# Dilated window attention beside a long convolution on one core: key offsets on partitions, v read back from DRAM at four shifts, sums by 32-column tiles, and spectra without a swapped copy

## The chip, the core and the metric

The kernel runs on one core of one Trainium2 chip. Time is device time in microseconds (us); each kernel was run several times, and the median stands with its range. The kernel before takes 244.41 us (three runs, 243.86 to 246.95). On the chips of the later runs its median lay between 244.3 and 247.2, so a kernel is compared with the runs of the kernel before on the same chip. A kernel that got a single look has one time, and its state (fast or slow) is unknown; it decides something only where the difference is far above the 1 to 2% by which runs scatter.

## The reference

Two independent parts share their length (S = 2048), their width (D = 576) and the output, where they stand side by side.

```python
# part A: 32 heads of 18, a causal window of 8 keys with step 2
qkv = x @ wqkv
idx = pos[:, None] - arange(8) * 2          # keys t, t-2, ..., t-14
logits = einsum(q, k[idx]) * 18 ** -0.5     # masked where idx < 0
o = einsum(softmax(logits), v[idx]);  a = o @ wo
# part B: a convolution of 4 taps, then one as long as the sequence, by FFT of length 4096
kv = (short convolution of k with shift_k) * v
y  = irfft(rfft(kv) * rfft(ssm_k))[:S] + kv * ssm_D;  b = q * y
out = concat(a, b)
```

## The kernel before

The engines each have a queue, and a written order (302 steps) says in which sequence the steps of A and B are issued. Three parts matter here.

**The weighted sum of v.** Times stand on the partitions (t = 16 a + b, with a on partitions). v is kept once in on-chip memory (`vX`), with a halo of 14 rows that is copied between partitions; the eight keys of a time are slots of the free axis. VectorE forms weight times v, and TensorE adds the eight products while it transposes them: each 128 x 128 block of products is loaded as weights and multiplied by the identity.

```python
def p_mul(tp, u):                                  # 16 of these
    vs = vX[:, t2:t2 + 15, :].rearrange(...)[:, 0:15:2]            # 8 keys, step 2
    nc.vector.tensor_tensor(P..., vs[:, :, 0:16], at.to_broadcast([128, W, 16, H]), ALU.mult)
    nc.vector.tensor_tensor(tails..., vs[:, :, 16:18], at.to_broadcast([128, W, 2, H]), ALU.mult)
def p_sum(tp, u):
    for ct in range(4):
        for wi in range(W):
            nc.tensor.matmul(oaccs[tp][:, u, ct, :], P[:, wi, 128 * ct:128 * ct + 128], ident[:], ...)
    # ... cut: the same for the tails
```

**The logit sum** multiplies products of q and shifted k by a 0/1 table on 32-column tiles of the array, four tiles at a time, reading its moving operand in runs of two elements (`prr[...][:, :, c, :, 2 * j:2 * j + 2]`).

**The spectra of B.** Transforms of the filter and of kv go out to DRAM (`Dk`, `Dx`) and come back with another axis on the partitions. A matmul makes 64 real and 64 imaginary rows at once. For the complex product, the filter's spectrum is also needed with its halves exchanged; two DMAs on GpSimd's queue make that copy.

```python
def by_rt(Dd, dh, g):
    return Dd[dh].rearrange("r (l h) d -> (r l) h d", h=32)[:, 8 * g:8 * g + 8, :]
def w_load(Dd, key, i):                            # 8 of Dk, 8 of Dx
    nc.sync.dma_start(Wr.get((key, i)), by_rt(Dd, i // 4, i % 4))
def k_spec(i):
    s2(Wr[("k", i)], i % 4, Kc[:, 0], 1.0 / 2048)
    nc.gpsimd.dma_start(Kc[0:64, 1], Kc[64:128, 0])
    nc.gpsimd.dma_start(Kc[64:128, 1], Kc[0:64, 0])
def g_prod(i, hv):
    nc.vector.tensor_tensor(Pp..., Kr[i][:, :, 4 * hv:4 * hv + 4, :], Xr[i]...to_broadcast([128, 2, 4, HD]), ALU.mult)
```

## Time and profile before

| | before |
|---|---|
| time, span of the profiled run | 244.41 us, 241.2 us |
| TensorE (PE) busy | 219.0 us, 91% of the span |
| VectorE (DVE) busy | 205.9 us, 85% |
| ScalarE (ACT) busy | 159.4 us, 66% |
| DMA | 55.24 MB, 229 GB/s over the span |

The prediction below shows the busy lines, stretches, groups and chain on which it was built. Two more views of the kernel before: the first is the busy time of the two halves (stretch, its length, then the busy time of each engine, the granted clock of TensorE as a share of full speed, the mean busy share of the 16 DMA engines, and GB/s). The second is the list of DMA issues, whose last column is the median time from issue to landing.

```profile
0.00:115.00 115.00, 104.73 (x807) 59.70 (x808) 102.40 (x125) 83.93 (x107) 11.04 (x38) 1.00 0.66 206
115.00:238.00 123.00, 114.32 (x1208) 88.96 (x1205) 103.47 (x108) 75.48 (x125) 14.52 (x24) 1.00 0.86 254
```

```profile
area<-Dk SPq DMA_DIRECT2D x8, 576.0 KB, 4.9
...
Dy<-area SPq DMA_DIRECT2D x8, 576.0 KB, 4.2
out_dram<-area SPq DMA_DIRECT2D x16, 288.0 KB, 4.4
```

In both halves TensorE is above 90%, and in the second the DMA engines are already busy 86% of the time.

### The profile page before, as it was taken

To read this page: it belongs to the slowest core of one execution; us is meant where nothing else is said; L and a number is where in the kernel's file an instruction comes from. 1 tells how busy PE (TensorE), PEld (TensorE's weight loads), DVE (VectorE), ACT (ScalarE), POOL (GpSimd) and SP (SyncE) were. 2 spreads that over 40 slices of the span, in tenths; PEclk is the share of its full clock that TensorE was granted. 3 is DMA by queue.
4 is the path that set the end of the run, shared out by engine and by line. 5 is a ranking of instruction groups with operands and counts; after the bars stand their busy time and mean duration, and the time that the engine had idled before them with its cause. 6 is when DMAs were issued, how large, how long until landed. Compare 5 with 4: busy or idle time off the path is not lost.

```text
span 241.2 us, 4997 instructions
## 1 busy us (share of the span) xinstructions
PE 219.0 (91%) x2013; PEld 148.7 (62%) x2013; DVE 205.9 (85%) x232; ACT 159.4 (66%) x231; POOL 25.6 (11%) x62
## 2 busy tenths in 40 slices
PE   1998999999996998999999779999899999999991
PEld 1444564446555544495684368768596779779770
DVE  1989999999988798998997999999999579974443
ACT  2777966779686777758837919858979682663030
POOL 8900000000000000000112010101120111111000
PEclk9999999999999999999999999999999999999998
DMA  6999994533435665557689887978879989879984
GB/s 206 323 339 388 362 288 146 157 101 99 134 91 169 196 195 148 169 141 281 192 226 283 273 237 257 269 246 272 181 258 284 280 237 281 273 227 283 282 241 147
DMA packets 44366, 55.24 MB, mean 229 GB/s; under 512 B 2316, under 2 KB 37468, under 8 KB 44344
## 3 DMA queue, kind: packets, MB, share of 16 engines
q1 hardware_dynamic: 42374, 47.71, 63.7%
q0 software_dynamic: 1968, 7.23, 11.2%
q8 instruction: 15, 0.25, 0.5%
q14 instruction: 7, 0.06, 0.1%
q10 hardware_dynamic: 2, 0.00, 0.0%
HBM read 29.27 MB, written 18.87 MB: 200 GB/s over the span
## 4 chain that ended last, share of the span: by engine, by line
PE 65%; DVE 12%; ACT 12%; DMA 6%; issue 4%; DVEq 0%; SPq 0%; ACTq 0%
PE psA L393 11%; ACT area L96 8%; PE psA L632 7%; PE psA L651 4%; PE psB L380 4%; DVE area L618 4%; PE psB L429 3%; PE psA L516 3%; PE psB L563 3%; PE psB L651 3%; PE psA L380 3%; PE psB L596 3%; PE psB L393 3%; ACT IAt L96 3%; DVE area L500 2%
## 5 line engine op out<-in xcount | busy, mean ns | idle before, releaser
L96 ACT ACTIVATE area<-psB 128x576 bf16<-128x576 f32 (+6 forms) x121 | 82.3, 714 | 33.6 <-PE psB L596 10.3
L96 ACT ACTIVATE area<-psA 128x576 bf16<-128x576 f32 (+7 forms) x94 | 66.9, 739 | 38.4 <-PE psA L651 11.6
L500 DVE TENSOR_TENSOR area<-area 128x2048 bf16<-128x2048 bf16 x32 | 38.0, 1224 | 2.9 <-PE psA L516 2.7
L618 DVE TENSOR_TENSOR area<-area,area 128x4096 bf16<-128x4096 bf16 x16 | 36.6, 2286 | 3.9 <-PE psA L632 3.3
L632 PE MATMUL psA<-ident,area 128*128 128x128 bf16 x512 | 34.0, 219 | 0.0
L632 PEld LDWEIGHTS <-area 128*128 128x128 bf16 x512 | 31.2, 98 | 1.8 <-DVE area L618 0.2
L393 PE MATMUL psA<-area,area 128*128 128x512 bf16 x120 | 31.3, 399 | 0.3 <-ACT area L96 0.3
L393 PEld LDWEIGHTS <-area 128*128 128x128 bf16 x160 | 15.5, 100 | 18.1 <-issue 1.9
L582 DVE TENSOR_TENSOR area<-area,area 128x2304 bf16<-128x2304 bf16 x16 | 21.5, 1355 | 2.6 <-DMA area<-area 1.1
L460 DVE TENSOR_TENSOR area<-area,area 128x2304 bf16<-128x2304 bf16 x16 | 21.3, 1353 | 0.6 <-DMA area<-in_B_k_dram 0.4
L574 POOL DMA_DIRECT2D area<-area x8 | 4.2, 527 | 159.0 <-DVE area L539 104.5
L380 PEld LDWEIGHTS <-area 128*128 128x128 bf16 x160 | 19.9, 144 | 1.2 <-issue 0.6
L563 PE MATMUL psB<-area,W 128*128 128x288 bf16 x96 | 18.0, 285 | 2.6 <-DVE area L98 1.6
L563 PEld LDWEIGHTS <-W 128*128 128x128 bf16 x128 | 11.9, 97 | 12.9 <-issue 10.0
L651 PEld LDWEIGHTS <-area 128*128 128x128 bf16 x160 | 15.5, 98 | 4.5 <-issue 0.6
L98 DVE CAST area<-psA 128x768 bf16<-128x768 f32 (+4 forms) x14 | 11.5, 834 | 6.3 <-PE psA L651 4.2
L429 PEld LDWEIGHTS <-T 128*128 128x128 bf16 x96 | 8.5, 98 | 12.9 <-issue 5.2
L465 DVE TENSOR_TENSOR area<-area 128x2304 bf16<-128x2304 bf16 x12 | 16.2, 1354 | 0.2
L596 PEld LDWEIGHTS <-IAt 128*128 128x128 bf16 x128 | 12.1, 97 | 6.6 <-issue 2.4
L429 PE MATMUL psB<-area,T 128*128 128x384 bf16 x60 | 14.0, 327 | 1.5 <-DVE area L290 1.2
L596 PE MATMUL psB<-area,IAt 128*128 128x288 bf16 x80 | 12.5, 285 | 1.0 <-DVE area L582 0.7
L651 PE MATMUL psA<-wv,area 128*128 128x288 bf16 x90 | 13.1, 286 | 0.0
(121 smaller groups left out, 287.3 us busy)
## 6 DMA issues: line engine op xcount, KB each, us to landing
Dx<-area SPq DMA_DIRECT2D x16, 288.0 KB, 3.0
Dk<-area SPq DMA_DIRECT2D x16, 288.0 KB, 3.1
area<-Dk SPq DMA_DIRECT2D x8, 576.0 KB, 4.9
area<-Dx SPq DMA_DIRECT2D x8, 576.0 KB, 4.6
area<-area POOLq DMA_DIRECT2D x16, 288.0 KB, 5.3
Dy<-area SPq DMA_DIRECT2D x8, 576.0 KB, 4.2
out_dram<-area SPq DMA_DIRECT2D x16, 288.0 KB, 4.4
area<-Dy SPq DMA_DIRECT2D x8, 576.0 KB, 6.3
```

Of the source, the lines that this page charges most:

```text
L96: nc.scalar.activation(dst, src, ACT.Copy, **({} if scale is None else {"scale": scale}))
L380: nc.tensor.matmul(ps[:, di, 0:288], xTt[:, kb, t2, :], wv[:, kb, d0:d1], start=(kb == 0), stop=(kb == 4))
L393: nc.tensor.matmul(ps[:, u, :], wcols(kb, comp, 2 * cp + u), xT[:, kb, t], start=(kb == 0), stop=(kb == 4))
L429: nc.tensor.matmul(ps[:, ri, 0:384], T1[:, ri, :], sf[:, 384 * ch:384 * ch + 384], start=True, stop=not extra)
L460: nc.vector.tensor_tensor(dst, kfull[:, 4 * c + 3 - j:4 * c + 7 - j, :], skb[:, j, :].unsqueeze(1).to_broadcast([128, 4, D]), ALU.mult)
L500: nc.vector.tensor_tensor(dst[:, u], halves(q2[h], hf), halves(k2[h][:, :, shs[u]:shs[u] + S], hf), ALU.mult)
L563: nc.tensor.matmul(ps[:, hp, 0:HD], W2[:, 8 * g + 2 * prl + hp].rearrange("p i l f -> p (i l f)"), Wt[:, 2 * prl + hp, :], start=True, sto ...
L582: nc.vector.tensor_tensor(Pp.get((i, hv)), Kr[i][:, :, 4 * hv:4 * hv + 4, :], Xr[i][:, 4 * hv:4 * hv + 4, :].unsqueeze(1).to_broadcast([12 ...
L596: nc.tensor.matmul(ps[:, hp, 0:HD], IAt[:, zi, 8 * g + hl, :], Pp[(i, hv)][:, zi, hl % 4, :], start=(zi == 0), stop=(zi == 1))
L618: nc.vector.tensor_tensor(P.rearrange("p w (d h) -> p w d h", h=H), vs[:, :, 0:16], at.to_broadcast([128, W, 16, H]), ALU.mult)
L632: nc.tensor.matmul(oaccs[tp][:, u, ct, :], P[:, wi, 128 * ct:128 * ct + 128], ident[:], start=(ct == 0 and wi == 0), stop=(wi == W - 1 and ...
L651: nc.tensor.matmul(ps[:, di, 0:288], lhs, wot[:, ct if ct < 4 else 4 + u, d0:d1], start=(ct == 0), stop=(ct == 4))
```

## The change

The intent: take work from TensorE, the fuller engine, and the swap copies from the DMA.

- The eight keys of the window are split as 2 x 4, and the four go on partitions: partition 32 j + h holds head h at key offset 2 j. v is projected with times on the free axis, written to a DRAM scratch `Dv`, and read back **four times, shifted by two elements each**. The weighted sum then is a sum over four partition groups, for which a 128 x 32 table and 32-column tiles are enough.
- The logit sum and the softmax follow that layout; the logit sum now reads its operand contiguously.
- The spectra run as pairs of half-array matmuls that put real and imaginary parts into different columns of the free axis, so that the exchanged halves are only another view, and the swap copies go.
- The fifth, half-empty block of the q, k and v projections runs in paired 64-row or 64-column tiles. The order is written anew, it is now forced on every engine, and the set-up (with 11 matmuls on zeros at the start) has become a part of it.

The core of the diff (the order, set-up, softmax and buffers are cut):

```diff
@@ v goes to DRAM and comes back
+    Dv = dram.tile([4 * D, VT], BF16, name="Dv")
+    def v_step(c, k):
+        # ... cut: projection with times on the free axis, evacuation into vT
+            nc.sync.dma_start(Dv[r0:r0 + 256, :].rearrange("(u p) t -> p u t", p=128), vT)
+    def v_load(c, k):
+        nd = 8 if k < 2 else 2
+        dst = (vSr if k < 2 else vStr).get((c, k))
+        sl = Dv[D * c + 8 * k:D * c + 8 * k + 1, 2:3]
+        nc.sync.dma_start(dst.rearrange("p d t -> p (d t)")[:, 0:nd * VT - 8],
+                          bass.AP(tensor=sl.tensor, offset=sl.offset, ap=[[DIL, 4], [DH * VT, 32], [1, nd * VT - 8]]))
-    def halo(c):
-        # ... cut
@@ the weighted sum
-        for ct in range(4):
-            for wi in range(W):
-                nc.tensor.matmul(oaccs[tp][:, u, ct, :], P[:, wi, 128 * ct:128 * ct + 128], ident[:], ...)
+                for wg in range(2):
+                    for dd in range(4):
+                        nc.tensor.matmul(ps[32 * dd:32 * dd + 32, u, :], I4[:], P[:, wg, dd, :], start=(wg == 0), stop=(wg == 1),
+                                         tile_position=(0, 32 * dd))
@@ spectra and their product
-        nc.gpsimd.dma_start(Kc[0:64, 1], Kc[64:128, 0])
-        nc.gpsimd.dma_start(Kc[64:128, 1], Kc[0:64, 0])
+            for im in range(2):
+                for hp in range(2):
+                    nc.tensor.matmul(ps[64 * hp:64 * hp + 64, im, 0:HD],
+                                     W2[:, im, 8 * g + 2 * prl + hp].rearrange("p l f -> p (l f)"),
+                                     Wt[:, 2 * prl + hp, :], start=True, stop=True, tile_position=(0, 64 * hp))
+        swap = bass.AP(tensor=K.tensor, offset=K.offset + K.ap[1][0], ap=[K.ap[0], [-K.ap[1][0], 2]] + ...)
+        nc.vector.tensor_tensor(P[:, 0:2], X, K, ALU.mult)
+        nc.vector.tensor_tensor(P[:, 2:4], X, swap, ALU.mult)
```

In `v_load` each pair is [step, count], the slowest first: 4 shifts of two elements, 32 heads, and then one contiguous run.

## The prediction

> **What bounds the kernel now.** I read the page's first part, then the busy time by stretches, then the chain of work in order of time for the real rate of each matmul, then the groups by shape, and last the DMA slices.
>
> First part of the page, and its slices:
>
> ```profile
> span 241.2 us, 4997 instructions
> PE 219.0 (91%) x2013; PEld 148.7 (62%) x2013; DVE 205.9 (85%) x232; ACT 159.4 (66%) x231; POOL 25.6 (11%) x62
> ...
> DMA packets 44366, 55.24 MB, mean 229 GB/s; under 512 B 2316, under 2 KB 37468, under 8 KB 44344
> ...
> HBM read 29.27 MB, written 18.87 MB: 200 GB/s over the span
> ```
>
> TensorE and VectorE are both nearly full. Busy time by stretches (columns: stretch, its length, PE, PEld, DVE, ACT, POOL, clock, DMA share, GB/s) says where each one loses time:
>
> ```profile
> 12.00:70.00 58.00, 56.39 (x421) 30.58 (x420) 56.81 (x54) 45.21 (x57) 0.22 (x1) 1.00 0.66 216
> 70.00:120.00 50.00, 46.38 (x402) 28.43 (x400) 44.38 (x55) 36.89 (x52) 1.06 (x2) 1.00 0.60 181
> 120.00:180.00 60.00, 55.26 (x588) 42.20 (x587) 57.54 (x59) 43.11 (x70) 8.30 (x14) 1.00 0.84 251
> 180.00:220.00 40.00, 38.84 (x420) 31.52 (x418) 32.59 (x31) 24.48 (x42) 5.16 (x8) 1.00 0.89 266
> 220.00:236.00 16.00, 15.15 (x165) 12.45 (x161) 6.91 (x10) 3.80 (x6) 0.00 (x0) 1.00 0.90 247
> ```
>
> DVE is 98% busy from 12 to 70 us and 96% from 120 to 180, but 81% from 180 to 220 and 43% from 220 to 236: there TensorE alone sets the pace. It works off the weighted sum, the output projection and the inverse transforms. The chain of work in order of time (start, us, what) confirms it and gives real matmul spacings, which the overlapping durations of the groups hide:
>
> ```profile
> 36.46 2.16 PE psA L393 x10
> 126.05 1.81 PE psA L516 x16
> 216.05 0.49 PE psB L671 x4
> 216.54 3.57 PE psA L632 x64
> ```
>
> So a 512-column matmul costs 216 ns, a 288-column one 123, a 128-column one 56, and one of the logit sum's 512-column matmuls on a 32-column tile (L516) 113. By the kernel's loops times these spacings, TensorE's stream in us is: transposes of x and of the filter 9.5, q and k projections 39 (160 and 20 of 216 ns), v 20, tables and bias 6, first transform 16 (96 of 163), logit sum 19, attention transposes 2, spectra 16, inverse 16, weighted sum 32 (576 of 56), projection 20, last transform 8. That is 202 of 241.
>
> VectorE's large groups (mean ns of one after the busy time):
>
> ```profile
> L500 DVE TENSOR_TENSOR area<-area 128x2048 bf16<-128x2048 bf16 x32 | 38.0, 1224 | 2.9 <-PE psA L516 2.7
> L618 DVE TENSOR_TENSOR area<-area,area 128x4096 bf16<-128x4096 bf16 x16 | 36.6, 2286 | 3.9 <-PE psA L632 3.3 <-ACT area L96 0.6
> L582 DVE TENSOR_TENSOR area<-area,area 128x2304 bf16<-128x2304 bf16 x16 | 21.5, 1355 | 2.6 <-DMA area<-area 1.1 <-issue 1.0 <-ACT area L96 0.2
> L460 DVE TENSOR_TENSOR area<-area,area 128x2304 bf16<-128x2304 bf16 x16 | 21.3, 1353 | 0.6 <-DMA area<-in_B_k_dram 0.4
> ```
>
> From 2048 to 4096 elements it adds 1062 ns, so a product costs about 162 ns plus 0.52 ns an element.
>
> [...] L516 shows only 216/113 = 1.9. But L516 reads its moving operand in runs of two elements. The 64-column table matmuls (L413) read it contiguously and keep the 219 ns duration of a full-array matmul, against 632 for L516 and 399 for a full-array 512. I therefore put the halved rate down to the strided read, an inference. [...] The trace's best 3 us stretch has 391, but late stretches with rows of 576 bytes have 220 to 340 at a share near one.
>
> **The change part by part, TensorE.** The weighted sum: 512 + 64 full-array matmuls of 128 columns (32 us) become 128 of 512 columns and 32 of 256 on 32-column tiles. With four tiles side by side that is 128 x 60 + 32 x 35 ns = 9 us (16 at L516's rate). The logit sum keeps its columns but reads them contiguously: 160 x 60 = 10 us instead of 19 (again 18 in the bad case). q and k: the fifth, half-empty block of two column groups runs as a pair of 64-row tiles, 9 x 216 instead of 10 x 216, so 39 becomes 36. v: 8 x 9 x 216 + 4 x 5 pairs of 256 columns = 18 instead of 20. Tables: 32 transposes, 2 instead of 5. Spectra and inverse: 256 half-array matmuls each instead of 128 whole ones. If two run together, they stay at 16 to 17 us each; if not, each gains up to 15. Transposing the weights back: 32 x 63 = 2 us new. Sum: 202 - 23 - 9 - 3 - 2 - 3 + 2 + 2 = 166, or about 182 with the tiles at L516's rate.
>
> **VectorE.** Logit products: 32 x 1.22 + 16 x 0.42 = 45.9 become 16 x 2.29 + 4 x 1.22 = 41.5. Weight times v: 16 x 2.29 + 16 x 0.42 = 43.3 become 16 x 2.29 + 4 x 1.22 = 41.5. Spectrum products: 16 x 1.355 = 21.7 become 32 of 1152 elements, 32 x 0.76 = 24.3 (the halves swapped by the view, not by a copy). Softmax 15 stays, without its mask addition. Last products: 8 of 16 now find their operand evacuated by ScalarE, 8 x 0.75 + 8 x 0.46 = 9.7 instead of 12. Evacuations that the new order gives it: 31 instead of 37, 22 instead of 28. Convolution 43 and set-up 12 stay. The durations sum to 221 before and 210 after. Before, 232 instructions overlapped by (221 - 206)/232 = 0.065 us each; with about 213 instructions 210 becomes 196 us busy. So VectorE hardly falls: 10 us.
>
> **ScalarE.** By the same count its evacuations rise from 165 to 173 us in durations, busy 159 to about 167. **DMA.** Out: 16 swap copies of 288 KB (4.7 MB) and the halo copies (2.1 MB). In: v written to DRAM 2.4 MB, v read four times 9.7 MB in rows of 8 KB, 0.2 of weights. 55.2 becomes 60.8 MB, and more of it in the second half: from about 120 us on 30.5 MB becomes 35.5.
>
> **What sets the end.** TensorE's 36 us come from where it alone was the bound (180 us on) and from 70 to 120, where the two alternated. VectorE becomes the bound with 196. It reached 96 to 98% where TensorE let it, the set-up now runs while the first loads are under way, and the last large product stands near the end of the order. With 4 us of it in the first 6 and in the last 6 us, and 96% between: 12 + 192/0.96 = 212. The span is some 3 us less than the median time here (241.2 against 244.4), but a fully balanced order may do a little better than 96%. I keep a span of 209 and a time of 212.
>
> **The rivals.** (1) DMA takes over in the second half: 35.5 MB at the 290 GB/s of late full stretches are 122 us, and with the 9.7 MB of v at 390 still 25.8/0.29 + 9.7/0.39 = 114, against some 92 for VectorE there. For it: shares of 0.84 to 0.90 already. Against it: DMA ended almost nothing in the chain of waits before, some loads begin earlier, and the swaps had the longest landings (5.3 us) for their size. It would make about 220 to 226. (2) The tiles don't run side by side[...]: TensorE stays at 182 or more and shares the bound with VectorE, 218 to 226. For it: L516's 1.9; against it: its strided read. [...] (4) Everything overlaps better than I assume and TensorE's spare time removes nearly all gaps of VectorE: 203.
>
> **Range and chances.** The main line is 212; rivals 1 and 2 pull up by 6 to 14, rival 4 down by 9. Hence 202 to 225. [...] faster 0.94, within 2% 0.04, slower 0.02.
>
> **What would show it.** Right: PE busy down by 20 to 45 us, DVE busy 192 to 200 and above 90% of the span, DVE dense after 180 us, the 32-column matmuls of 512 spaced near 60 ns, products of 4096 still at 2.29 us and of 1152 at 0.76, the chain with more DVE than PE. Wrong: products waiting for DMA out of the v scratch (rival 1), 113 ns spacings and PE above 90% busy (rival 2)[...].

Passages are cut: statements about the hardware that no trace or run shows, and with them a whole rival, (3), which put the time at 245 to 260 us. Two premises of the 166 were estimates, which the trace of the kernel before doesn't show. One is that four tiles of 32 columns run side by side, at 60 ns for 512 columns and 35 for 256; "only" 1.9 and "the halved rate" are measured against it. (In the kernel after, 512 columns took 54 and 62 ns, and eight matmuls of 256, L687, 0.43 us or 54 ns each, at a granted clock of 0.50.) The other is that a pair of half-array tiles takes about as long as one full-array matmul. (The pairs later took 320 ns against 216 and 156 against 108 in the projections, and 138 to 152 against 123 in the spectra and inverses.)

## The result and the profile after

The changed kernel is correct and takes **313.22 us** (median of four runs, 312.44 to 314.99), against 244.69 for the kernel before on the same chip (four runs). The ratio is 1.279, with an interval of 1.269 to 1.290. Ratios in this document are the mean time of one kernel's fast runs over the mean of the other's fast runs of the same rounds, so they are not quite the ratio of the medians quoted. Executions over 1.5% slower than the fastest of the same kernel are left out of the means. The prediction, 212 with a range of 202 to 225, was wrong in size and in sign.

The first part of the page of the kernel after:

```profile
span 310.7 us, 4428 instructions
PE 209.2 (67%) x1726; PEld 108.3 (35%) x1736; DVE 197.9 (64%) x208; ACT 167.2 (54%) x239; POOL 16.0 (5%) x47
...
DMA packets 47061, 60.79 MB, mean 196 GB/s; under 512 B 2272, under 2 KB 40160, under 8 KB 46016
```

Every engine has less or little more work than before, and none is above 67%: nothing computes more, everything waits. The same two halves show where (columns as before):

```profile
0.00:115.00 115.00, 105.42 (x746) 51.24 (x757) 100.08 (x108) 82.64 (x108) 10.07 (x39) 0.99 0.68 219
115.00:305.00 190.00, 102.68 (x972) 56.34 (x972) 95.63 (x98) 83.92 (x132) 5.95 (x8) 0.76 0.61 183
```

The first 115 us are as before, within 3 us of busy time on each of the three main engines. The second half takes 190 us instead of 123, with less work for TensorE and VectorE than it had. The granted clock of TensorE is down to 0.76 only in that half, in which TensorE is idle nearly half of the time; in the second halves of later runs it was 0.67, 0.89, 0.94 and 0.96 where TensorE was busy 38, 78, 84 and 81% of the time. Whether one follows from the other, no run tests. The waits by engine and line (total us, times, longest) and the chain of work in order of time (start, us, what) name what is waited for. L661 is the product of weights and v, and L613 the spectrum matmul:

```profile
DVE area L661 <- DMA area<-Dv: 34.7, 5, 21.0
PE psB L613 <- DMA area<-Dx: 33.9, 3, 15.8
```

```profile
119.66 12.46 DMA area<-Dk
...
135.08 23.65 DMA area<-Dx
...
176.16 27.11 DMA area<-Dx
...
211.04 23.11 DMA Dy<-area
...
259.56 25.06 DMA out_dram<-area
```

The transfers on the end-setting chain are not only those of v. They are loads of `Dk` and `Dx` and stores of `Dy` and of the output, whose form the change left as it was. Their median landing was 4 to 5 us before; three of the four are shown below as they are now (the median of `Dx` is only 5.7, but single loads of it take 23 to 27 us on the chain):

```profile
area<-Dk SPq DMA_DIRECT2D x8, 576.0 KB, 18.1
Dy<-area SPq DMA_DIRECT2D x8, 576.0 KB, 19.7
out_dram<-area SPq DMA_DIRECT2D x16, 288.0 KB, 8.3
```

And yet the DMA engines are busy only 61% of the second half. The view of the DMA in 40 slices, for the stretch of the longest wait (176 to 203 us; busy tenths of the 16 engines, then GB/s), resolves the contradiction:

```profile
DMA  4993398944999922222222222222222222222598
GB/s 174 414 373 132 140 243 274 281 105 102 182 293 248 203 76 89 105 97 110 98 120 100 125 100 112 100 100 112 100 125 100 112 101 98 98 101 109 143 231 289
```

For 23 slices in a row, some 16 us, the share stands at 0.2 to 0.3 and the rate at 100 GB/s. A share of 0.25 is 4 of 16 engines, each at 25 GB/s, or all sixteen a quarter of the time. The packets of the trace decide: counted one by one, exactly four are in flight for 74 of the 190 us. So, by my reading, four engines work through a long backlog while twelve stand idle, and a transfer whose other parts have long landed waits for its share on the four. The trace doesn't name the engine of a packet.

**The theory.** `v_load` has 4 outermost on its source, and four packets are in flight while the backlog stands. I take the first for the cause of the second, and the four engines for the same ones in every load of v. This trace alone doesn't show that; the experiments test it.

An estimate from numbers of the traces, if all loads of v use the same four engines: the reads of v are 8 x 1054 + 4 x 262 KB = 9.7 MB, at 100 GB/s 97 us. The second half moves 190 x 183 = 34.8 MB, so the other 25.1 MB, spread over all engines at the 276 GB/s that the first experiment will show, take another 91 us on each of the four. Together that is 188 us, against the 190 of the second half.

Against this, the parts of the prediction about compute can be read in the groups of the kernel after (busy us, mean ns of one; then idle time before them) and in the chain:

```profile
L661 DVE TENSOR_TENSOR area<-area,area 128x4096 bf16<-128x4096 bf16 x16 | 36.2, 2287 | 32.4 <-DMA area<-Dv 32.1 <-DVE area L370 0.2
L635 DVE TENSOR_TENSOR area<-area,area 128x1152 bf16<-128x1152 bf16 x16 | 12.0, 750 | 0.0
```

```profile
68.80 0.78 PE psA L417 x10
81.11 0.88 PE psA L562 x16
...
164.14 1.10 PE psA L648 x16
...
294.57 0.98 PE psA L677 x16
```

The products run in 2287 and 750 ns, as predicted (2.29 and 0.76 us). Sixteen logit matmuls (L562) take 0.86 to 0.88 us, 54 ns each, and sixteen of the weighted sum (L677) 0.98 us, 62 ns each (predicted 60). The paired tiles are less good. Ten of v's tail (L417) take 0.78 us, which is 156 ns a pair, and sixteen of the inverse (L648) 1.10 us, which is 138 ns a pair where a full-array matmul took 123.

### The profile page after: what moved, and what is told of

It is laid out like the page before. It is cut to its first block, busy times and chain, and to the rows that moved or that the text cites. A ratio compares the mean times of both kernels' runs of the same rounds, so it can differ in the third digit from the quotient of the medians.

```text
span 310.7 us, 4428 instructions
## 1 busy us (share of the span) xinstructions
PE 209.2 (67%) x1726; PEld 108.3 (35%) x1736; DVE 197.9 (64%) x208; ACT 167.2 (54%) x239; POOL 16.0 (5%) x47
## 2 busy tenths in 40 slices
DMA packets 47061, 60.79 MB, mean 196 GB/s; under 512 B 2272, under 2 KB 40160, under 8 KB 46016
## 4 chain that ended last, share of the span: by engine, by line
PE 44%; DMA 40%; ACT 8%; DVE 2%; issue 2%; SPq 1%; ACTq 0%; DVEq 0%
DMA area<-Dx 16%; PE psA L391 10%; DMA out_dram<-area 8%; DMA Dy<-area 7%; ACT area L102 7%; DMA area<-Dk 4%; PE psB L472 4%; PE psB L391 3%; PE psB L613 3%; DMA area<-Dv 3%; PE psA L700 2%; PE psA L394 2%; PE psA L648 2%; PE psA L443 2%; ACT IAt L102 2%
## 5 line engine op out<-in xcount | busy, mean ns | idle before, releaser
L102 ACT ACTIVATE area<-psB 128x576 bf16<-128x576 f32 (+5 forms) x121 | 85.6, 746 | 69.4 <-PE psB L613 25.0
L102 ACT ACTIVATE area<-psA 128x576 bf16<-128x576 f32 (+6 forms) x105 | 75.2, 743 | 55.6 <-DMA out_dram<-area 23.1
L661 DVE TENSOR_TENSOR area<-area,area 128x4096 bf16<-128x4096 bf16 (+1 forms) x20 | 40.9, 2073 | 35.0 <-DMA area<-Dv 34.7
L613 PE MATMUL psB<-area,W 128*64 128x288 bf16 x176 | 21.1, 344 | 54.6 <-DMA area<-Dx 33.9
L613 PEld LDWEIGHTS <-W 128*64 128x64 bf16 x256 | 16.3, 122 | 66.8 <-issue 49.4
L540 DVE TENSOR_TENSOR area<-area 128x4096 bf16<-128x4096 bf16 x16 | 36.0, 2283 | 0.3 <-PE psB L562 0.2
L501 DVE TENSOR_TENSOR area<-area,area 128x2304 bf16<-128x2304 bf16 x16 | 21.2, 1352 | 2.2 <-PE psB L472 2.1
L634 DVE TENSOR_TENSOR area<-area,area 128x1152 bf16<-128x1152 bf16 x16 | 12.0, 748 | 16.5 <-ACT area L102 16.4
L677 PE MATMUL psB<-area,I 128*32 128x512 bf16 x64 | 5.0, 443 | 21.0 <-ACT area L102 21.0
L391 PEld LDWEIGHTS <-area 128*128 128x128 bf16 x128 | 12.1, 98 | 13.7 <-issue 0.9
L648 PEld LDWEIGHTS <-IAt 64*128 64x128 bf16 x256 | 13.0, 104 | 7.8 <-issue 2.7
L677 PEld LDWEIGHTS <-I 128*32 128x32 bf16 x128 | 3.2, 101 | 34.1 <-DVE area L661 23.7
L700 PEld LDWEIGHTS <-area 128*128 128x128 bf16 x128 | 11.1, 104 | 8.6 <-issue 3.9
L635 DVE TENSOR_TENSOR area<-area,area 128x1152 bf16<-128x1152 bf16 x16 | 12.0, 750 | 0.0
L648 PE MATMUL psA<-area,IAt 64*128 64x288 bf16 x144 | 11.3, 300 | 0.2
L677 PE MATMUL psA<-area,I 128*32 128x512 bf16 x64 | 5.2, 440 | 9.0 <-ACT area L102 8.9
## 6 DMA issues: line engine op xcount, KB each, us to landing
area<-Dk SPq DMA_DIRECT2D x8, 576.0 KB, 18.1
Dy<-area SPq DMA_DIRECT2D x8, 576.0 KB, 19.7
```

The lines of the kernel that those rows point to most:

```text
L102: nc.scalar.activation(dst, src, ACT.Copy, **({} if scale is None else {"scale": scale}))
L391: nc.tensor.matmul(ps[:, u, :], w[:, kb, cols[u]:cols[u] + 128], xT[:, kb, t], start=(kb == 0), stop=False)
L501: nc.vector.tensor_tensor(bufs[j], kfull[:, 4 * c + 3 - j:4 * c + 7 - j, :], skb[:, j, :].unsqueeze(1).to_broadcast([128, 4, D]), ALU.mult)
L540: nc.vector.tensor_tensor(prr.get((n, h)), q2[h][:, :, 512 * aq:512 * aq + 512].unsqueeze(1).to_broadcast([128, 4, 2, 512]), kv, ALU.mult)
L613: nc.tensor.matmul(ps[64 * hp:64 * hp + 64, im, 0:HD], W2[:, im, 8 * g + 2 * prl + hp].rearrange("p l f -> p (l f)"), Wt[:, 2 * prl + hp, ...
L634: nc.vector.tensor_tensor(P[:, 0:2], X, K, ALU.mult)
```

## The experiments

Twelve kernels ran. Their numbers of lines shift by a few; the text says which line is which. In the expectations, e1 is the first experiment (four transfers of 32 partitions), b4 the first try with four outermost, and e10 the kernel with two shifts copied by VectorE.

### v in four transfers of 32 partitions

The theory: the four outermost are the cause. The rival: the 9.7 MB themselves are. This kernel moves the same bytes to the same places in the same order, but each of the four shifts is a transfer of its own with 32 outermost.

```diff
-        nc.sync.dma_start(dst...[:, 0:nd * VT - 8],
-                          bass.AP(..., offset=sl.offset, ap=[[DIL, 4], [DH * VT, 32], [1, nd * VT - 8]]))
+        for j in range(4):
+            nc.sync.dma_start(flat[32 * j:32 * j + 32],
+                              bass.AP(..., offset=sl.offset + DIL * j, ap=[[DH * VT, 32], [1, nd * VT - 8]]))
```

> The changed kernel with each load of v from the scratch split into four transfers of 32 partitions, whose source has 32 as its outermost count; same bytes, same addresses, same result, 48 issues instead of 12. Theory A (the load's source has an outermost count of 4, so it runs on 4 of the 16 DMA engines at about 100 GB/s in all, and every later transfer of the queue waits behind it on those four): the stalls on Dx, Dk, Dy and output transfers vanish, DVE is again dense, 207 to 220 us. Rival B (the 9.7 MB, or reading the same rows four times at shifts of 4 bytes, is what DRAM can't deliver): nothing changes, 295 to 315 us. Rival C (the second half of the new order is bad in itself): 260 or more.

Measured: correct, **246.40 us** (245.94 to 247.00, four runs), before on this chip 244.28; ratio 1.010 (1.0055 to 1.0146). In the profile the second half:

```profile
115.00:240.00 125.00, 97.61 (x977) 54.79 (x976) 96.09 (x100) 83.27 (x131) 5.95 (x8) 0.89 0.95 276
```

```profile
138.63 10.20 DMA area<-Dk
...
157.94 12.38 DMA area<-Dk
```

The form of one access pattern is worth 0.269 in the ratio, 66 us. But the kernel is still no faster than the one before: my 207 to 220 us were missed, and the 212 us of the prediction are still 34 away. The reason is in the same line. With all engines in use their share is 0.95 at 276 GB/s, and 34.5 MB (125 x 276) fill the 125 us. The chain still waits for loads, of 10 to 12 us now. This looks like the rival (1) of the prediction, hidden until now behind the other fault; the run with a quarter of the bytes tests it.

### The unsplit loads on GpSimd's queue

The rival to four slow engines: not the engines, but the order of the one queue holds the other loads up behind those of v. Here the loads keep their four shifts in one transfer but are issued by GpSimd, with `nc.gpsimd.dma_start` in place of `nc.sync.dma_start`.

> The changed kernel with the unsplit loads of v issued by GpSimd, so in another queue than all other large transfers. If the harm is the order within one queue, the others now pass the loads of v: 225 to 255 us. If it is the time of the four engines themselves (9.7 MB at 100 GB/s are 97 us of them, beside their quarter of the other 26 MB, 89 us at 290 GB/s, in a half that took 190 us), a queue of its own helps little: 285 to 315 us. Rival B: 295 to 315.

Measured in one look (state unknown): 304.72 us, correct. Another queue doesn't help, which speaks against mere order. But the profile is not that of four busy engines. For 170 to 230 us, in the same view as above:

```profile
DMA  7796930045899999999999899978687688987899
GB/s 298 154 280 240 359 137 25 0 196 203 294 181 199 190 160 186 157 202 172 226 164 139 176 195 203 184 162 175 136 156 141 116 124 183 156 99 121 233 340 365
```

From about 185 us on the engines are mostly busy and yet move some 100 to 230 GB/s, and a load of v lands after 35 us (median). So a time in the expected range came about in another way, and I don't count this run as support for the four engines. What slows a transfer of this form on that queue stays open.

### v with two outermost

If the count outermost sets the number of engines, then two transfers with 2 outermost use two engines, for the same bytes.

```diff
+        for j in range(2):
+            nc.sync.dma_start(flat[64 * j:64 * j + 64],
+                bass.AP(..., offset=sl.offset + 2 * DIL * j, ap=[[DIL, 2], [DH * VT, 32], [1, nd * VT - 8]]))
```

> The changed kernel with each load of v split into two transfers of 64 partitions whose source has 2 as its outermost count. Theory A, if both halves land on the same two engines: 9.7 MB at 50 GB/s are 194 us, with their share of the rest 283 us after the first 115, so 370 to 410 us; if the halves land on two different pairs, about as the changed kernel, 300 to 320. Rivals B and C: 305 to 316, no change.

Measured in one look (state unknown): **398.74 us**, correct. The second half:

```profile
115.00:390.00 275.00, 104.39 (x965) 56.77 (x964) 94.68 (x97) 83.66 (x131) 5.95 (x8) 0.67 0.40 125
```

Here too the slices show it, for 170 to 230 us:

```profile
DMA  1116111111111117311111111111159821991111
GB/s 49 54 63 216 46 49 54 45 56 56 56 45 56 56 56 318 127 56 50 56 56 56 56 56 56 56 45 56 56 208 283 319 84 56 202 215 40 56 45 56
```

Two of sixteen engines are a share of 0.125, and exactly two packets are in flight for 162 of the 275 us. The time is the one expected if both halves of a load use the same two engines. The estimate made as above, 9.7 MB at 50 GB/s and 25.1 MB at 276, is 194 + 91 = 285 us; the half took 275. With 32 outermost it took 125, with 4 it took 190 and with 2 it took 275. A rival of bytes, queue or schedule has no reason to follow this count.

### The kernel before with four outermost, first try

If the outermost count is the cause, it should slow a kernel without any scratch for v too. In the kernel before, the 16 loads of `Dk` and `Dx` were written as 4 x 32 rows instead of 128.

```diff
+        (s0, n0), *rest = [list(d) for d in src.ap]
+        nc.sync.dma_start(Wr.get((key, i)), bass.AP(..., ap=[[32 * s0, 4], [s0, 32]] + rest))
```

> The kernel before with one thing added: the eight loads each of Dk and Dx (9.4 MB, at the same addresses, same result) are described with 4 x 32 rows instead of 128 in the source. Theory A: they fall to four engines, 95 us or more of those engines beside a quarter of the rest, in a kernel that has no v scratch at all: 275 to 320 us and landings of 8 us or more instead of 4.9. Rivals B and C: 243 to 247, nothing changes. If the description is merged back to 128 rows on the way to the chip, nothing changes either and the run tells nothing.

Measured in one look: 249.93 us, correct, and the loads land in 5.6 and 4.6 us. This tells nothing about the cause. The two counts, which together make up evenly spaced rows, had been merged back into one of 128 in the program that was built; the landings fit that. The experiment had failed in its making.

### The kernel before with four outermost, second try

The same loads with rows in another order, 4 x 32 with a long inner step, can't be merged. The rows arrive permuted. Its output is wrong, which doesn't matter for the time. The comparison with the reference still passed, so its tolerance doesn't see this part of the output well.

```diff
+        nc.sync.dma_start(Wr.get((key, i)), bass.AP(..., ap=[[s0, 4], [4 * s0, 32]] + rest))
```

> The kernel before, with the 16 loads of Dk and Dx described as 4 x 32 rows in a permuted order that can't be merged into 128 (the attempt b4 was merged back to 128 rows in the program, so it told nothing). Same bytes, the same rows of 4.6 KB, a wrong result on purpose. Theory A (an outermost count of 4 means four engines): 9.4 MB at 100 GB/s are 94 us of those four, beside a quarter of the other 21 MB of this stretch, 72 us at 290 GB/s: 166 us or more from 107 us on, 265 to 310 us, landings of 6 us or more. If the outermost count isn't the cause: 243 to 247.

Measured in one look (state unknown): **318.87 us**, where the kernel before took 247.24 on that chip. The chain:

```profile
130.41 18.67 DMA area<-Dx
...
180.68 21.45 DMA area<-Dx
...
248.67 20.03 DMA area<-Dx
```

From 176 to 203 us the slices are these:

```profile
DMA  2993222473322272229999513222222222222222
GB/s 109 389 416 157 102 109 109 135 208 97 96 72 92 73 232 84 89 109 239 205 212 225 116 72 111 82 97 101 90 101 102 96 109 109 109 102 96 104 108 102
```

A kernel with none of the change but this form of access pattern is slowed just as much, a little over what I had expected, and stands at 0.2 to 0.3 and 100 GB/s again (exactly four packets in flight for 70 us after 115). That settles the first cause. The run also corrects me on a detail: these loads have contiguous rows of 4.6 KB (8 x 288 elements), not the rows of 576 bytes that I had put down for late loads.

### A quarter of v's bytes

How much of what remains is bytes? From the kernel with four transfers of 32 rows, only the first quarter of each row is read: 7.3 MB fewer, wrong (relative error 1.08), with the same count of transfers and rows.

```diff
+        m = (nd * VT - 8) // 4
-              ... ap=[[DH * VT, 32], [1, nd * VT - 8]]))
+              ... ap=[[DH * VT, 32], [1, m]]))
```

> The kernel with v split by 32 rows (e1, 246 us), but each of its loads of v brings only the first quarter of its columns: 48 transfers as before, 2.4 MB instead of 9.7. The result is wrong on purpose. If the second half of e1 is bound by what the DMA engines can move (34.5 MB at 276 GB/s are 125 us, which is what it took), 7.3 MB less take 26 us off: 216 to 226 us. If it is bound by the order of the transfers in the one queue, or by their number, nothing or little changes: 240 to 248.

Measured in one look (state unknown): 233.63 us, on a chip where the kernel before took 247.24 (0.945 of it). By its ratio of 1.010, the parent would have taken 249.7 there, so the bytes are worth 16 us, not the 26 that 7.3 MB need at 276 GB/s. The time lies between my two ranges: bytes matter, but by less than they would if they alone bound the half.

```profile
115.00:228.00 113.00, 95.28 (x978) 53.92 (x977) 96.07 (x101) 83.31 (x131) 5.96 (x8) 0.94 0.78 242
```

The DMA no longer fills the half (0.78), and still VectorE is at 96.07/113 = 85% and TensorE at 84%. So about 20 us of the miss are still there with a quarter of v's bytes.

### Without the forced order

The change also forces the written order on every engine. Rival: the order is what harms. From the four transfers of 32 rows, with `with tc.manual_schedule(engines=None):` replaced by `if True:`.

> The kernel e1 without the forced order of the list, so that the scheduler may move instructions. If the forced order is what makes the second half slow (rival C), 225 to 240. If DMA bytes are its bound: 240 to 265, no gain.

Measured in one look (state unknown): 256.39 us, correct, before 247.24. That is about 2.7% above the 249.7 us worked out for its parent on this chip, so the forcing isn't the harm. Whether another written order would do better, no run shows.

### Two shifts read, two copied by GpSimd

Half of the shifts can be made on chip: partitions 64 to 127 hold the same data as 0 to 63, shifted by four elements.

```diff
+        for j in range(2):
+            nc.sync.dma_start(flat[32 * j:32 * j + 32, 0:n + 4],
+                bass.AP(..., offset=sl.offset + DIL * j, ap=[[DH * VT, 32], [1, n + 4]]))
+        nc.gpsimd.tensor_copy(flat[64:128, 0:n], flat[0:64, 4:n + 4])
```

> The kernel e1, with only the first two key offsets (64 partitions) read from the scratch; GpSimd copies them to the other 64 partitions, shifted by 4 elements. Same result, 4.85 MB less DMA in the second half. If DMA is its bound: 17 us less, 226 to 234 us, the first version faster than the kernel before. If GpSimd's copies are slower than some 8 us each or hold VectorE up, or if the order of the queue is the bound: 240 to 260.

Measured: correct, 258.62 us (257.35 to 260.48); ratio 1.049 (1.040 to 1.058). 4.8 MB fewer, and by the ratios (1.049 against 1.010) some 9 us slower than with four reads. The groups show what became slower; L665 is the product of weights and v, and L639 the spectrum product with exchanged halves:

```profile
L665 DVE TENSOR_TENSOR area<-area,area 128x4096 bf16<-128x4096 bf16 x16 | 47.5, 2991 | 0.3 <-DMA area<-Dv 0.2
...
L434 POOL COPY area<-area 64x4216 bf16<-64x4216 bf16 x8 | 35.1, 4404 | 43.6 <-DMA area<-Dv 43.6
...
L639 DVE TENSOR_TENSOR area<-area,area 128x1152 bf16<-128x1152 bf16 x16 | 18.9, 1184 | 0.0
```

VectorE's products went from 2287 to 2991 ns and from 750 to 1184 on average, and its busy time from 197 to 227 us. The twelve copies, 40 us in all, start at 120 us or later. The logit products of 4096 elements, of which the last starts at 119 us in the kernel after, keep 2283 ns here. How a copy slows a product is not shown: the other half of the spectrum products (L638), in the same stretch, keeps 741 ns.

### Four transfers of 32 rows on GpSimd's queue

Do the many small loads harm because they stand in the same queue as all others? The first experiment with `nc.gpsimd.dma_start`.

> The kernel e1, but its 48 loads of v are issued by GpSimd, in a queue of their own, so the loads of Dk, Dx and Dy don't stand behind 1 MB of v. Same bytes. If the order within one queue costs what the byte count doesn't explain (cutting the bytes to a quarter gained only 16 us): 228 to 240 us. If the engines' total work is the bound: 243 to 252.

Measured: correct, 259.75 us (256.81 to 260.58); ratio 1.054 (1.044 to 1.064). My expectation was missed. The waits of GpSimd, where L431 is the issue of a load and L663 the product that frees its buffer:

```profile
POOL area L431 <- DVE area L663: 46.9, 3, 35.0
```

GpSimd, which has other loads behind, stands 47 us for free buffers, and the DMA reaches only 250 GB/s in the second half. The queue is no remedy.

### Two shifts read, two copied by VectorE

The copy can also be made by VectorE, in 12 instructions right before the products that need it. As in the kernel with GpSimd's copies, but:

```diff
-        nc.gpsimd.tensor_copy(flat[64:128, 0:n], flat[0:64, 4:n + 4])      # after the load
+        if ct % 2 == 0:                                                     # in p_mul, before the product
+            nc.vector.tensor_copy(flat[64:128, 0:n], flat[0:64, 4:n + 4])
```

> The kernel e1 with two of the four key offsets read and the other two copied by VectorE just before the first product that uses them (12 copies, an estimated 12 us in all), instead of by GpSimd, whose copies raised VectorE's products of 4096 from 2.29 to 2.99 us and its busy time by 30 us. If DMA is the bound and VectorE has room: 234 to 243 us, faster than the kernel before by 0 to 5%. If VectorE's 12 us cost as much as the transfers they replace: 244 to 254. Products of 4096 back at 2.29 us.

Measured: correct, **237.96 us** (236.23 to 238.47), before on this chip 245.64; ratio 0.966 (0.960 to 0.973). This is faster than both kernels. The copies (L665) and the products (L668), and the second half:

```profile
L668 DVE TENSOR_TENSOR area<-area,area 128x4096 bf16<-128x4096 bf16 x16 | 36.2, 2288 | 0.6
...
L665 DVE COPY area<-area 64x4216 bf16<-64x4216 bf16 x8 | 10.0, 1252 | 0.3
```

```profile
115.00:233.00 118.00, 95.56 (x980) 53.15 (x979) 109.29 (x113) 84.15 (x133) 7.26 (x8) 0.96 0.85 255
```

A copy that GpSimd made in 4404 ns takes VectorE 1252, and the products are back at 2288. VectorE is now at 109.29/118 = 93% of the second half and the DMA at 0.85.

### The kernel before with the new spectra alone

The other part of the change by itself: half-array spectra and inverses, no swap copies, the written order as it was.

```diff
-        nc.gpsimd.dma_start(Kc[0:64, 1], Kc[64:128, 0])
-        nc.gpsimd.dma_start(Kc[64:128, 1], Kc[0:64, 0])
+            # s2, g_prod, g_inv, tables and buffers as in the changed kernel
```

> The kernel before with only the spectrum part of the change: half-array spectra and inverse, no swapped copies (4.7 MB of GpSimd's transfers out), products of 1152. By the prediction's terms TensorE gains up to 2 us and loses 3 in the tables, VectorE gains 2.6: 240 to 248 us. If the pairs of half-array matmuls don't run together, TensorE gains up to 15 us and the time becomes 250 to 262.

Measured: correct, 261.14 us (260.24 to 264.32; the slowest run is left out of the ratio), before 245.64; ratio 1.060 (1.053 to 1.068). The DMA falls to 50.55 MB, but TensorE, the fullest engine there, has 228.7 us busy instead of 219.0. Its chain (L564 spectrum, L599 inverse):

```profile
211.48 0.61 PE psB L564 x8
...
227.97 1.21 PE psA L599 x16
```

A pair takes 152 ns in both, against 123 ns for the full-array matmul that it replaces. So the time fell into the range given for pairs that don't run together, but not for that reason: one after the other, two would take 246. For 256 pairs that is 256 x 29 = 7 us of the 16. The rest I didn't trace to a part: the old order was tuned for the old steps, and time is lost in the first half too. This part of the change by itself isn't a gain.

### Less projection work

The last question: what keeps VectorE from the density of 96% that the prediction gave it? In the kernel after itself, the stretches from 30 to 100 us:

```profile
30.00:70.00 40.00, 39.79 (x215) 16.87 (x217) 36.20 (x30) 31.94 (x43) 2.48 (x4) 1.00 0.51 157
70.00:100.00 30.00, 29.75 (x235) 14.59 (x237) 25.85 (x19) 22.13 (x30) 1.70 (x6) 1.00 0.59 180
```

TensorE is busy 99% and VectorE 89%. If TensorE sets the pace there, then less work for it must shorten the kernel. From the kernel with VectorE's copies, one of four full blocks of the q and k projections is dropped: 32 matmuls of 216 ns, 6.9 us. Its output is wrong, which doesn't matter for the time.

```diff
-            for kb in range(4):
+            for kb in range(3 if w is wq else 4):
```

> The kernel e10 (238 us), with one of the four full blocks of the contraction left out of every q and k projection: 32 matmuls of 512 columns less, 32 x 0.216 = 6.9 us of TensorE in the first 115 us, where it is 99% busy from 30 to 110 us and VectorE only 90%. The result is wrong on purpose; no other engine's work changes. If TensorE still bounds that half (so that the prediction's 96% for VectorE could not come about there): 231 to 234 us. If VectorE or the order bounds it: 236 to 240.

Measured: **231.51 us** (230.07 to 233.30), before on this chip 244.50; ratio 0.950 (0.944 to 0.957), where its parent had 0.966 (0.960 to 0.973). The same stretch of the trace:

```profile
30.00:70.00 40.00, 38.80 (x221) 16.82 (x223) 39.44 (x32) 34.11 (x46) 2.91 (x5) 1.00 0.58 174
```

VectorE now does 39.44 us of work in these 40, where its parent did 36.11. From 70 to 100 us it is less dense, 27.01 of 30 against 25.89. The last logit matmul of the first half comes 6 us earlier, and the time falls by 1.6%, 3.9 us. TensorE bounds the stretch up to about 115 us, and part of what is won there is lost again in the second half.

## Why the prediction was wrong

In shares of the kernel before, so that the chips agree, the miss divides as follows; one hundredth is 2.4 us.

| step | ratio | difference in us |
|---|---|---|
| predicted | 212/244.41 = 0.867 | |
| v by 32 rows, a quarter of its bytes (one look) | 0.945 | 19 |
| v by 32 rows, all bytes | 1.010 | 16 |
| the kernel after | 1.279 | 66 |

**What was right.** VectorE's work: 197.9 us busy, predicted 196, with its products at the predicted durations, 2287 and 750 ns. ScalarE's: 167.2, predicted 167. The bytes: 60.79 MB, predicted 60.8, and 34.8 MB in the second half (from 115 us), predicted 35.5 (from about 120). The 32-column tiles run side by side, at 54 and 62 ns where 60 was predicted and a full-array matmul takes 216 (3.5 to 4.0 times as fast), so rival (2) is out. The inference that the logit sum had been slow because of its strided read fits: the same tile with a contiguous read went from 113 to 54 ns, though no run changed the read alone.

**What was off in size only.** TensorE's pairs of tiles. A pair in v's tail takes 156 ns instead of 108 (half of 216), a pair of 512 columns in the projections 320 in the chain instead of 216, a pair of the inverse 138 and one of the spectra 152 instead of 123. Against two full-array matmuls in sequence the pairs are 1.4 times as fast in the projections and 1.6 to 1.8 times in the spectra and inverses. With 20, 24, 128 and 128 such pairs, TensorE's stream is 1.0 + 2.5 + 1.9 + 3.7 = 9 us longer than the predicted 166, an estimate from these spacings. Its busy time fell to only 209.2 us, outside the predicted fall of 20 to 45, although that figure is a poor measure of the stream: with the same matmuls it was 203.6 in the kernel with four transfers of 32 rows, where the clock was 0.94 instead of 0.84. The prediction's list for the kernel before adds up to 203.5 and not to 202; nothing hangs on it.

**The step that failed** is the one on DMA, "v read four times 9.7 MB in rows of 8 KB", with its use in rival (1) as "the 9.7 MB of v at 390". I costed the loads by bytes and by length of rows. I didn't look at the outermost count of the access pattern, though it stood in the diff. The loads ran with four packets in flight, at 100 GB/s, and the others, which by my reading have a part on each of these four engines too, were slowed with them: loads of `Dk` from 4.9 to 18.1 us, stores of `Dy` from 4.2 to 19.7. The three kernels with 32, 4 and 2 outermost (246, 313 and 399 us) and the kernel before with 4 (319 instead of 247) show it. Cost: 66 us.

**The second step** that failed is the choice among rivals. Rival (1), the DMA taking over the second half, was given as 114 to 122 us for that half and 220 to 226 for the whole. With the first fault mended the half takes 125 us at a share of 0.95: the mechanism was right, and the rate was 276 GB/s instead of 290 and 390. The 390 was wrong in kind: by the durations of its packets, v's rows of 8.4 KB moved at 231 GB/s there and all the rest at 318 (bytes over packet time, times 16 engines, an estimate). The long rows were the slow ones; why is not shown. What I held against it, that the DMA ended almost nothing in the chain of the kernel before, was true of a kernel in which the second half lasted 123 us for 31 MB anyway. It said nothing of one in which TensorE no longer stretched the half. A quarter of the bytes brings back 16 us.

**The third** is "96% between". It compared each engine's total over the whole kernel, 166 us against 196, and concluded that VectorE would set the pace throughout. But the bound changes between the halves. The prediction's own list has some 97 us of TensorE's work before the weighted sum begins (transposes 9.5, q and k 36, v 18, tables and bias 3, first transform 16, logit sum 10, attention transposes 4), so an imbalance of the totals could not help the first half: TensorE is 99% busy from 30 to 100 us. Removing 6.9 us of it made VectorE dense from 30 to 70 us and the kernel shorter, which shows it. Of the 19 us that remain, the trace of the kernel with a quarter of v's bytes (span 231.9, VectorE busy 196.8) leaves VectorE idle 6 us in the first 30, 8 between 30 and 100, 17 in the second half to 228 and 4 at the end. What fills the 17 us, waits of the chain for the first shifted loads and a last stretch in which TensorE sets the pace, is read from the trace and not tested. That part stays open.

## What to carry to other kernels

Before a transfer is costed by its bytes, look at the outermost count of its source's access pattern: on the sync queue, a count of 4 kept four packets in flight here, at 100 GB/s, and a count of 2 kept two, at about 50; other transfers then waited, by my reading, for their own shares on those engines. The mark in this profile was long landings of transfers that weren't touched (18.1 us instead of 4.9 for `Dk`), at a low DMA share that stood at a round fraction (0.2 to 0.3, four of sixteen). Balance engines stage by stage and not by their totals, and when one engine is relieved, check what the transfers of that stage need at full rate: here that was the next bound, a share of 0.95 at 276 GB/s.
